# A fused attention, routing and expert kernel: the end of the attention phase in another order

## The chip, the cores and the metric

One core of a Trainium2 chip runs the whole program. The metric is the device time of an execution in microseconds. Five engines work in it, each through its own instructions in order: TensorE (PE; PEld is its weight load), VectorE (DVE), ScalarE (ACT), GpSimd (POOL) and SyncE (SP), which here issues most DMA transfers. They wait for each other through semaphores.

## The reference, cut

Three stages, each with the output of the one before as its input. First a gated linear attention over 4 batches, 8 heads, 768 positions, 40 values a head:

```python
m_new = np.maximum(f_gate[:, :, t] + m, i_gate[:, :, t])
C = f_stab * C + i_stab * np.einsum('bhd,bhe->bhde', vt, kt)
n = f_stab * n + i_stab * kt
h_tilde = np.einsum('bhde,bhe->bhd', C, qt)
denom = np.maximum(np.abs(nq), 1.0)
y[:, :, t] = sigmoid(o_gate) * h_tilde / denom
```

Then a mixture of 8 experts on the 3072 tokens of 320 values, where each token goes to one expert, and a gated layer with 1536 hidden values:

```python
e_idx = np.argmax(x @ w_gate, axis=1)
out[mask] = gate_w * eom * (np.maximum(x[mask] @ w1[e], 0.0) @ w2[e])
return (sigmoid(x @ w_gate) * (x @ w_val)) @ w_out
```

## The kernel before, in words

The tokens are cut into 24 chunks of 128 (six chunks a batch). The attention runs as a pipeline of steps: `step(n)` goes through the names in the table `ORDER` (lines 40 to 43), each with a lag, and calls the part of that name for chunk n minus lag. All five engines run in the order in which the code issues (a manual schedule). For a chunk the parts are, in the order in which its data needs them: `dec`, `exp`, `sc`, `pf` (the products of queries and keys with their decay), `kw`, `inter`, `state`, `C`, `Cm`, `cb` (the running state), `gs` and `out` (the chunk's result in PSUM), `abs` and `den` (the denominator and its reciprocal), `th` (ScalarE, tanh of the output gate), `th1` (adds one to it, line 743, 128x320 in float32), `sod` (GpSimd: gate times reciprocal), `x` (VectorE), `xh`, `xla`, `xl` (the row as a high and a low half: ScalarE, GpSimd, VectorE), `tr` and `ev` (five transposes and their copy out of PSUM), `log` and `lg` (the logits).

When the logits of a group of chunks are there (groups of 6, 6, 4, 5 and 3 chunks), `route` (line 783) computes for its tokens the expert, the row within the expert's list and the gate, as a generator of small pieces, most of them VectorE ops, which `r` entries of `ORDER` pull one by one; a piece that yields `True` ends the entry, since the next one waits for another engine. Its one-hot table (L802) goes to TensorE (L806, L808), whose counts the later pieces read. Behind it the chunk's rows are `pending`, and `scatter` (line 848) writes the rows of one chunk into the experts' lists in DRAM by an indirect DMA that GpSimd issues (L850), one a step at `scat`, and more through `out_of` in later steps.

The first 16 chunks choose the first expert (the one with most tokens), and its first 256 rows are handled by a job of its own, `Head`: its rows are loaded by a transposing DMA (L337, with the small L338 behind it) once the scatters of the first 16 chunks have landed, `sums` (L879 on VectorE, L880 on ScalarE) adds their halves, `up` (L888) makes 24 float32 matmuls, three for each of eight blocks of hidden values, with a relu on ScalarE behind each block (L890), and `down` (L894) makes 16. `load_weights` loads that expert's weights through SP in six blocks, at the steps that `LOADS` names, and `convert` splits them into halves for the expert's remaining rows (L111 on ScalarE, L112 on VectorE). SP also writes blank rows behind the expert's list (`blank_rows`, L101).

Before, steps 1 to 25 run; steps 24 and 25 finish the last chunks with what is left of `ORDER`. In step 23 the early rows' load is issued, in step 24 `sums` and the first 12 matmuls of `up`. Then `tail` runs the route of chunks 16 to 20 to its end, the pending scatters, `tr`, `ev`, `log` and `lg` of chunks 21, 22 and 23 one after the other, the last route, `sort_experts`, the last scatters, the conversion and `down`. The remaining rows of the first expert follow as the next job: its matmuls (L125) need the second load of rows, which waits for all scatters and for `sort_experts`. The other experts and the gated layer come behind.

## Time and profile before

| | |
|---|---|
| median of 3 runs | 727.23 us (726.78 to 731.73) |
| the profiled execution: its time, its span | 726.39 us, 724.3 us |
| TensorE busy, matmuls | 698.8 us (96%) |
| VectorE busy | 396.7 us (55%) |
| ScalarE busy | 328.1 us (45%) |
| GpSimd busy | 144.8 us (20%) |
| mean granted TensorE clock | 0.981 |

The span runs from the first to the last instruction; times within it count from its start. "Busy" is the time in which an engine worked on an instruction; TensorE's matmuls are pipelined and their ends are modelled, so that a busy TensorE need not be at its peak. The granted clock is TensorE's, 1.00 being 2.4 GHz. A wait is named by the instruction that ended it.

### The profile page before, as it was taken

The page shows a single profiled execution, that of the slowest core. Times are in us where ns is not written, and L with a number is a line of the kernel's source. Part 1 is how long each engine was busy: PE and PEld are TensorE (multiplying, and loading weights), DVE is VectorE, ACT ScalarE, POOL GpSimd, SP SyncE. Part 2 cuts the span into 40 slices and gives each one's busy share as a digit, 9 for nine tenths or more (in the row PEclk, how much of TensorE's full clock was granted, in tenths as well). Part 3 has the DMA queues.
Part 4 walks back from the last instruction along what each step waited for, and adds up shares of the span by engine and source line. Part 5 has one row for each costly group of instructions (what it writes and reads, how often), then busy time and mean ns, then how long its engine had stood idle before and what let it go on. Part 6 is the DMA issues. An engine that isn't in the chain of part 4 may idle for free. (4 is left out here: it accounts for less than half of the span.)

```text
span 724.3 us, 15451 instructions
## 1 busy us (share of the span) xinstructions
PE 698.8 (96%) x6048; PEld 495.2 (68%) x6048; DVE 396.7 (55%) x912; ACT 328.1 (45%) x782; POOL 144.8 (20%) x172
## 2 busy tenths in 40 slices
PE   8899999869999999999989999999999999999998
PEld 5799998857666775667656676666666666666665
DVE  6767678627788879898877810322403223032230
ACT  5477787625575666654545511322313223132231
POOL 5456788842211121221100000000000000000000
PEclk8799999988999999999999999999999999999999
DMA  6466667543999998873525013001020020000000
GB/s 192 130 183 178 199 185 215 174 143 87 273 297 292 266 274 234 253 232 108 139 59 138 21 35 76 0 19 37 1 55 1 10 47 1 28 1 10 19 0 28
DMA packets 67131, 84.02 MB, mean 116 GB/s; under 512 B 41401, under 2 KB 48970, under 8 KB 67058
## 3 DMA queue, kind: packets, MB, share of 16 engines
q1 hardware_dynamic: 63824, 73.35, 36.1%
q0 software_dynamic: 2640, 9.33, 3.6%
q8 instruction: 48, 0.79, 0.5%
q10 hardware_dynamic: 594, 0.35, 0.2%
q14 instruction: 25, 0.20, 0.1%
HBM read 57.53 MB, written 17.16 MB: 103 GB/s over the span
## 5 line engine op out<-in xcount | busy, mean ns | idle before, releaser
L125 PE MATMUL pa<-xT,wgv 128*128 128x384 f16 x1536 | 250.9, 326 | 2.8 <-DVE hh L1166 2.1
L125 PEld LDWEIGHTS <-wgv 128*128 128x128 f16 x1536 | 150.2, 98 | 102.2 <-issue 3.4
L1161 DVE SCALAR_TENSOR_TENSOR gt<-pa,sg 128x384 f32<-128x384 f32 x96 | 53.5, 557 | 224.2 <-PE pa L125 193.3
L1179 PE MATMUL pb<-wo,hh 128*128 128x320 f16 x864 | 118.5, 299 | 0.0
L1160 ACT ACTIVATE sg<-pa 128x384 f32<-128x384 f32 x96 | 47.0, 490 | 143.7 <-PE pa L125 143.7
L1179 PEld LDWEIGHTS <-hh 128*128 128x128 f16 x864 | 84.5, 98 | 33.2
L358 PE MATMUL pb<-w,hh 128*128 128x320 f16 (+4 forms) x624 | 86.6, 299 | 0.0
L125 PE MATMUL pa<-xT,w 128*128 128x384 f16 (+5 forms) x576 | 80.9, 301 | 1.6 <-DVE hh L348 1.6
L358 PEld LDWEIGHTS <-hh 128*128 128x128 f16 (+4 forms) x624 | 62.8, 101 | 22.3 <-DVE hh L348 0.5
L125 PEld LDWEIGHTS <-w 128*128 128x128 f16 x640 | 55.7, 98 | 32.6 <-issue 2.6
L112 DVE SCALAR_TENSOR_TENSOR w<-ws,w 128x512 f16<-128x512 f32 (+1 forms) x92 | 56.1, 642 | 4.7 <-ACT w L111 3.9
L111 ACT ACTIVATE w<-ws 128x512 f16<-128x512 f32 (+1 forms) x92 | 50.3, 592 | 13.1 <-DMA ws<-in_w 11.7
L1181 ACT ACTIVATE ob<-pb 128x320 f32<-128x320 f32 x24 | 10.5, 437 | 100.5 <-PE pb L1179 100.5
L660 PE MATMUL ps<-qk 128*128 128x128 f32 x384 | 53.9, 287 | 0.0
L1166 DVE TENSOR_TENSOR hh<-gt,hh 128x384 f16<-128x384 f32 x96 | 52.7, 549 | 0.7
L369 POOL DMA_INDIRECT y_d<-yr,own x24 | 28.0, 1167 | 125.0 <-ACT w L111 19.5
L1165 ACT ACTIVATE hh<-gt 128x384 f16<-128x384 f32 x96 | 49.4, 515 | 5.9 <-DVE gt L1161 5.9
L660 PEld LDWEIGHTS ps<-qk 128*128 128x128 f32 x384 | 49.9, 203 | 1.0 <-issue 0.2
L665 DVE TENSOR_TENSOR pf<-ps,w 128x512 f32<-128x512 f32 x48 | 33.0, 686 | 21.7 <-ACT w L655 11.4
L347 ACT ACTIVATE hh<-pa 128x384 f16<-128x384 f32 (+6 forms) x80 | 33.4, 431 | 13.8 <-PE pa L125 13.1
L348 DVE SCALAR_TENSOR_TENSOR hh<-pa,hh 128x384 f16<-128x384 f32 (+6 forms) x80 | 36.3, 480 | 3.9 <-ACT hh L347 3.6
L655 ACT ACTIVATE w<-pw 128x512 f32<-128x512 f32 x48 | 28.3, 592 | 1.4 <-PE pw L651 0.5
(185 smaller groups left out, 716.5 us busy)
## 6 DMA issues: line engine op xcount, KB each, us to landing
ws<-in_w SPq DMA_DIRECT2D x24, 512.0 KB
vk<-in_vk SPq DMA_DIRECT2D x24, 324.0 KB
qk<-in_qk SPq DMA_DIRECT2D x48, 160.0 KB
ws<-in_w SPq DMA_DIRECT2D x15, 480.0 KB
ws<-in_wg SPq DMA_DIRECT2D x9, 512.0 KB
ws<-in_wv SPq DMA_DIRECT2D x9, 512.0 KB
ws<-in_wo SPq DMA_DIRECT2D x8, 480.0 KB
out<-ob SPq DMA_DIRECT2D x24, 160.0 KB
```

Source lines behind the costliest of these rows:

```text
L111: A.activation(hi, src, AF.Copy, scale=scale)
L112: low = lambda: V.scalar_tensor_tensor(lo, src, scale, hi, ALU.mult, ALU.subtract)
L125: PE.matmul(ps, r if swap else l, l if swap else r, start=n == 0, stop=n == len(steps) - 1)
L347: A.activation(self.hh[:, 0, f], ph, AF.Relu)
L348: V.scalar_tensor_tensor(self.hh[:, 1, f], ph, 0.0, self.hh[:, 0, f], ALU.max, ALU.subtract)
L358: PE.matmul(py, self.hh[:, x, k, sl], w2[:, y, k, :], start=k == 0 and x + y == 0, stop=k == K1 - 1 and x == 1)
L660: PE.matmul(m.ps[g][:, p, :], m.k2[:, g, p], m.q2[:, p], start=True, stop=True)
L1160: A.activation(sg, pgv[0], AF.Sigmoid, scale=1.0 / (SY * SWG))
L1161: V.scalar_tensor_tensor(gt, pgv[1], SGT / (SY * SWV), sg, ALU.mult, ALU.mult)
L1165: A.activation(self.gh[:, 0, f, :], box[0], AF.Copy)
L1166: V.tensor_sub(self.gh[:, 1, f, :], box[0], self.gh[:, 0, f, :])
L1179: PE.matmul(po, self.gh[:, x, k, sl], wo[:, y, k * DM:(k + 1) * DM], start=k == 0 and x + y == 0, stop=k == K2 - 1 and x == 1)
```

## The change

- `th1` (line 743) runs on VectorE instead of GpSimd, for all 24 chunks.
- From step 17 on a second scatter a step is issued behind `xla`; the extra ones behind `kw` and `sod` of the last steps are gone, and `r` and `scat` are no longer left out in step 23.
- The early rows' load is issued in step 22, behind `xl`'s place, and with it the blank rows' write, which before came in step 24. `LOADS` puts the third, fourth and fifth block of weights in step 23 (before 23, 24, 24), the sixth in `tail` (before step 25). `sums` runs at the end of step 23.
- Steps 24 and 25 are gone. `tail` is written out: what is left of the chunks 21 to 23 (`c`, `d`, `e`), pieces of the route of chunks 16 to 20 and single matmuls of `ups` in turn. `up(n)` issues n matmuls, `r(n)` n pieces of a route, `posts()` the relus due.

```diff
         def th1(m):
-            G.tensor_scalar_add(gate(m.t)[:, 0], gate(m.t)[:, 0], 1.0)
+            V.tensor_scalar_add(gate(m.t)[:, 0], gate(m.t)[:, 0], 1.0)
...
-            def up(self, f):
...
-                return lambda: A.activation(self.hh[:, f], ph, AF.Relu, scale=SW1 * SW2)
+            def ups(self):
+
+                for f in range(K1):
...
+                    for k in range(3):
+                        PE.matmul(ph, step.ws[k][:, 128 * f:128 * (f + 1)], self.x32[:, k], start=k == 0 and f % 2 == 0, stop=k == 2,
+                                  skip_group_check=True)
+                        if k == 2:
+                            step.posts.append(lambda f=f, ph=ph: A.activation(self.hh[:, f], ph, AF.Relu, scale=SW1 * SW2))
+                        yield
...
-                    if n == NTILE - 1 and name == "xl":
-
+                    if n == NTILE - 2 and name == "xl":
+
+                        assert not pending
                         mem = Within(hids[0], psS, psC, ("pw", "c"))
                         step.job = Head(mem, step.row, HEAD, lambda ins: tc.add_to_no_dep_group("first rows", ins.ins))
+
+                        blank_rows(first_end(), SLOTS[0] - HEAD)
                     parts[name](chunks[n - lag])
...
-                    if n >= (NTILE - 1 if name != "sod" else 20) and name in ("kw", "sod", "xla"):
+                    if n >= 17 and name == "xla":
                         out_of(1)
...
+            if n == NTILE - 1:
+                step.job.sums()
...
+            c, d, e = chunks[-3:]
...
+            load_weights(5)
+            th(e)
+            gs(e)
+            sod(d)
+            tr(c)
+            ev(c)
+            th1(e)
+            r(2)
+            for g in range(2):
+                out_(e, g)
+            log(c)
+            lg_(c)
+            x(d)
+            abs_(e)
+            den(e)
+            xh(d)
+            up(2)
+            r(3)
+            sod(e)
+            xla(d)
+            xl(d)
+            r(3)
+            up(3)
+            x(e)
+            xh(e)
+            r(4)
+            xla(e)
+            xl(e)
+            tr(d)
+            ev(d)
+            up(2)
+            tr(e)
+            log(d)
+            lg_(d)
+            for _ in step.route:
+                pass
+            ev(e)
             out_of(len(pending))
...
+            up(2)
+            log(e)
+            lg_(e)
+            r(5)
+            up(3)
+            posts()
+            r(3)
+            up(3 * K1)
+            for _ in step.route:
                 pass
             sort_experts()
             out_of(len(pending), True)
+            posts()
             convert(len(step.pieces))
...
-        LOADS = {21: [0], 22: [1], 23: [2], 24: [3, 4], 25: [5]}
+        LOADS = {21: [0], 22: [1], 23: [2, 3, 4]}
...
-            for n in range(1, NTILE + 2):
+            for n in range(1, NTILE):
                 step(n)
             tail()
```

What stands on the engines now, at three places. First GpSimd's own order in steps 21 and 22. L850 is a scatter, L673 `kw`, L758 `xla`, L743 `th1`, L737 `sod`. Before, from `kw` of step 21 on:

```order
L673 TENSOR_TENSOR kw_113<-vk,tm 128x8x40
L850 DMA xs_d<-xsb,dest 29824x322
L758 TENSOR_TENSOR xsb<-x,xsb 128x256
L743 TENSOR_SCALAR hh<-hh 128x320
L737 TENSOR_TENSOR sod<-hh,den 128x320
L850 DMA xs_d<-xsb,dest 29824x322
L673 TENSOR_TENSOR kw_112<-vk,tm 128x8x40
L850 DMA xs_d<-xsb,dest 29824x322
```

And in the change:

```order
L673 TENSOR_TENSOR kw_113<-vk,tm 128x8x40
L850 DMA xs_d<-xsb,dest 29824x322
L758 TENSOR_TENSOR xsb<-x,xsb 128x256
L850 DMA xs_d<-xsb,dest 29824x322
L737 TENSOR_TENSOR sod<-hh,den 128x320
L673 TENSOR_TENSOR kw_112<-vk,tm 128x8x40
L850 DMA xs_d<-xsb,dest 29824x322
```

`th1` is gone from this engine, and a scatter stands in its place behind `xla`; the one behind `sod` is gone.

Then SP's queue in steps 22 and 23: L432 loads a chunk's values, L910 (L913 in the change) a block of the first expert's w1, L337 and L338 the early rows, L917 (L920) a block of its w2, L101 writes the blank rows. Before:

```order
L432 DMA vk<-in_vk 128x648
L910 ISA
L910 DMA ws<-in_w 128x1024
L910 ISA
L910 DMA ws<-in_w 128x1024
L337 ISA
L337 DMA_TRANSPOSE hh<-xs_d 128x5x256
L338 ISA
L338 DMA hh<-xs_d 128x2x2
L917 ISA
L917 DMA ws<-in_w 128x960
```

And in the change:

```order
L913 DMA ws<-in_w 128x1024
L337 ISA
L337 DMA_TRANSPOSE hh<-xs_d 128x5x256
L338 ISA
L338 DMA hh<-xs_d 128x2x2
L250 TENSOR_LOAD first_i
L250 ISA x2
L101 ISA
L101 DMA xs_d<-fill 128x2x322
L913 ISA
L913 DMA ws<-in_w 128x1024
L920 ISA
```

The early rows' load has moved ahead of the third block of w1, and the blank rows' write stands between the two.

Last, TensorE around the last route: L888 (L889 in the change) are matmuls of the hidden layer of the first 256 rows, L806 and L808 the counts of the last route, L894 (L897) the output matmuls of those rows. Before:

```order
L888 MATMUL pa<-hh,ws 128x256 x3
L806 LDWEIGHTS c_74
L806 MATMUL pr<-oh,c_74 128x24
L808 LDWEIGHTS c_74
L808 MATMUL pr<-oh,c_74 128x24
L808 LDWEIGHTS c_74
L808 MATMUL pr<-oh,c_74 128x16
L808 LDWEIGHTS c_74
L808 MATMUL pr<-oh,c_74 128x8
L888 MATMUL pa<-hh,ws 128x256 x3
L894 MATMUL pb<-ws,hh 128x320 x3
```

And in the change:

```order
L889 MATMUL pa<-hh,ws 128x256 x3
L806 LDWEIGHTS c_74
L806 MATMUL pr<-oh,c_74 128x24
L808 LDWEIGHTS c_74
L808 MATMUL pr<-oh,c_74 128x24
L808 LDWEIGHTS c_74
L808 MATMUL pr<-oh,c_74 128x16
L808 LDWEIGHTS c_74
L808 MATMUL pr<-oh,c_74 128x8
L889 MATMUL pa<-hh,ws 128x256 x12
L897 MATMUL pb<-ws,hh 128x320 x3
```

Twelve of the 24 hidden-layer matmuls stand behind the last route now, where three did.

## Rows read from the trace of the kernel before

**Rows 1.** Busy time by stretch: us, then the engines, TensorE's granted clock, DMA.

```profile
142.40:147.80 5.40, 1.14 (x34) 1.03 (x33) 1.75 (x4) 0.84 (x5) 1.73 (x2) 0.96 0.74 115
147.80:151.00 3.20, 3.18 (x8) 2.63 (x9) 1.84 (x7) 0.49 (x3) 2.41 (x3) 0.54 0.56 226
...
161.00:164.00 3.00, 0.08 (x2) 0.00 (x0) 0.00 (x0) 0.89 (x2) 1.17 (x4) 0.50 0.30 110
164.00:167.50 3.50, 3.46 (x19) 2.74 (x20) 1.48 (x9) 1.07 (x5) 0.00 (x0) 0.50 0.02 5
...
177.50:724.30 546.80, 539.06 (x3665) 353.21 (x3664) 277.13 (x567) 213.92 (x460) 35.09 (x28) 1.00 0.35 99
```

**Rows 2.** Order of time, step 23 on: start us, us, engine, line [idle before <-releaser].

```profile
142.46 0.51 DVE L698 TENSOR_TENSOR po<-po,tm 128x328 f32<-128x328 f32 x1
...
142.71 1.49 SPq L337 DMA_TRANSPOSE hh<-xs_d  x1
...
143.02 1.13 PE L683 MATMUL po<-vk,pf 128*64 128x41 f32 x32 [0.61 <-DVE po L698]
...
147.02 0.69 DVE L879 TENSOR_TENSOR hh<-hh 128x512 f32<-128x512 f16 x1 [2.14 <-DMA hh<-xs_d]
...
148.89 0.15 DVE L732 TENSOR_SCALAR den<-den 128x8 f32<-128x8 f32 x1
...
151.47 0.71 POOL L758 TENSOR_TENSOR xsb<-x,xsb 128x256 f16<-128x256 f32 x1 [1.10 <-ACT xsb L755]
...
154.67 2.84 PE L888 MATMUL pa<-hh,ws 128*128 128x256 f32 x12
...
157.34 0.44 PE L767 MATMUL pt<-c,xsb 128*128 128x128 f16 x5
...
158.98 0.18 ACT L778 ACTIVATE lg<-pl 128x16 f32<-128x16 f32 x1 [0.45 <-PE pl L125]
...
163.28 0.70 ACT L771 ACTIVATE xTu<-pt 128x640 f16<-128x640 f16 x1 [2.04 <-remote]
...
164.68 0.18 DVE L792 TENSOR_REDUCE m<-lg 128x3 f32<-128x24 f32 x1 [8.74 <-ACT lg L778]
...
165.54 0.18 DVE L802 TENSOR_TENSOR oh<-rk,m 128x24 f16<-128x24 f32 x1
...
167.13 1.87 PE L888 MATMUL pa<-hh,ws 128*128 128x256 f32 x6
...
168.84 1.78 PE L894 MATMUL pb<-ws,hh 128*128 128x320 f32 x6
...
177.54 7.15 PE L125 MATMUL pa<-hh,w 128*128 128x256 f16 x64
```

**Rows 3.** GpSimd's groups from 120 to 138 us: busy us, mean ns | idle.

```profile
L743 POOL TENSOR_SCALAR hh<-hh 128x320 f32<-128x320 f32 x4 | 4.1, 1014 | 0.1
L758 POOL TENSOR_TENSOR xsb<-x,xsb 128x256 f16<-128x256 f32 x4 | 2.7, 687 | 1.1 <-ACT lg L778 0.7 <-ACT m L817 0.3
...
L737 POOL TENSOR_TENSOR sod<-hh,den 128x320 f32<-128x320 f32 x3 | 2.2, 722 | 0.2
```

**Rows 4.** Order of time in steps 22 and 23, columns as in rows 2.

```profile
136.26 1.03 POOL L850 DMA_INDIRECT xs_d<-xsb,dest  x1 [0.17 <-issue]
...
136.64 0.68 DVE L732 TENSOR_SCALAR den<-den 128x8 f32<-128x8 f32 x1
...
138.05 0.28 PE L767 MATMUL pt<-c,xsb 128*128 128x128 f16 x2 [0.59 <-POOL xsb L758]
...
139.94 1.05 POOL L850 DMA_INDIRECT xs_d<-xsb,dest  x1 [0.16 <-issue]
```

**Rows 5.** Two lines by themselves: ns min/median/max, first and last start, forms.

```profile
L732 DVE TENSOR_SCALAR den<-den x24: 149/392/677, 28.6 to 148.9; 128x8 f32<-128x8 f32 x24
L1097 DVE TENSOR_SCALAR u<-ws x26: 403/419/591, 227.3 to 414.9; 128x512 uint32<-128x512 uint32 x18, 128x480 uint32<-128x480 uint32 x8
```

**Rows 6.** VectorE's group of `pf` from 40 to 138 us: busy, mean ns | idle.

```profile
L665 DVE TENSOR_TENSOR pf<-ps,w 128x512 f32<-128x512 f32 x39 | 26.8, 686 | 14.7 <-ACT w L655 10.2 <-PE pw L651 3.8 <-issue 0.3
```

More of the change, by code (lines that the diff above doesn't have):

```diff
@@ L859, in routing @@
             for _ in range(k):
-                if next(step.route, None) and not step.drain:
+                if next(step.route, None):
                     break
@@ L880, in sums @@
                 A.activation(self.x32[:, 2], self.xT[:, 2], AF.Copy)
-            def up(self, f):
-                if f % 2 == 0:
-                    self.both = psS.tile([128, NP * T], F32, name="pa", tag=("pw", "ps")[f // 2 % 2]).rearrange("p (f n) -> p f n", f=2)
-                ph = self.both[:, f % 2]
-                for k in range(3):
-                    PE.matmul(ph, step.ws[k][:, 128 * f:128 * (f + 1)], self.x32[:, k], start=k == 0 and f % 2 == 0, stop=k == 2,
-                              skip_group_check=True)
-                return lambda: A.activation(self.hh[:, f], ph, AF.Relu, scale=SW1 * SW2)
+            def ups(self):
+                for f in range(K1):
+                    if f % 2 == 0:
+                        both = psS.tile([128, NP * T], F32, name="pa", tag=("pw", "ps")[f // 2 % 2]).rearrange("p (f n) -> p f n", f=2)
+                    ph = both[:, f % 2]
+                    for k in range(3):
[4 more added lines that the diff above has]
+                        yield
             def products(self, w2, i, py):
@@ L927, in step @@
         def step(n):
-            step.drain = n >= NTILE
             if n == 3:
@@ L958, in step @@
                         to_end(1)
-                    if n >= (NTILE - 1 if name != "sod" else 20) and name in ("kw", "sod", "xla"):
+                    if n >= 17 and name == "xla":
                         out_of(1)
-                    if n == NTILE and name == "x":
-                        step.job.sums()
-                    if n == NTILE and name == "out1":
-                        step.posts, step.done = [step.job.up(f) for f in range(4)], 0
+            if n == NTILE - 1:
+                step.job.sums()
@@ L966, in tail, with up @@
         def tail():
-            def ups(n):
+            step.posts = []
+            ups = step.job.ups()
+            c, d, e = chunks[-3:]
+            def up(n):
                 for _ in range(n):
-                    step.posts.append(step.job.up(len(step.posts)))
-            def posts(n):
-                for p in step.posts[step.done:n]:
-                    p()
-                step.done = n
-            stops = 0
-            for stop in step.route:
-                if stop:
-                    stops += 1
-                    if stops == 2:
-                        ups(UPS - len(step.posts))
-                        posts(2)
@@ L984, in tail, with posts @@
-            out_of(len(pending))
-            for t in (NTILE - 3, NTILE - 2, NTILE - 1):
-                tr(chunks[t])
-                ev(chunks[t])
-                log(chunks[t])
-                if t == NTILE - 2:
-                    posts(UPS - 2)
-                lg_(chunks[t])
-            ups(1)
-            posts(UPS)
-            for stop in step.route:
-                pass
-            ups(1)
-            posts(K1)
+                    next(ups, None)
+            def posts():
+                while step.posts:
+                    step.posts.pop(0)()
@@ new lines, in r @@
+            def r(n):
+                for _ in range(n):
+                    next(step.route, None)
+            load_weights(5)
[17 more added lines that the diff above has]
+            sod(e)
```

15 lines of the change are left out of this document (5 added, 10 removed).

## The prediction, before the run

> **What bounds the kernel now.** I read the table of stretches first. From 177.5 us to the end TensorE is busy 539.06 of 546.80 us at a granted clock of 1.00; ahead of that it has holes, with 1.14 us of work in the 5.40 from 142.4 on and 0.08 in the 3.00 from 161 on [rows 1]. So what follows the attention runs at TensorE's pace, and the change can only move the moment at which that long stretch begins: the first matmul of the first expert's remaining rows (L125), at 177.54 [rows 2]. The profiled execution took 726.39 us, which is 177.54, plus 546.8 behind it, plus some 2.1 outside the span.
>
> Then I read the order of time from step 23 to 177.54 [rows 2], as one chain. Chunk 23's `gs` (L698) starts at 142.46 and its `out` matmuls (L683) end at 144.15. Then VectorE sits 2.14 us in front of `sums` (L879, 147.02), because the first expert's rows, asked for at 142.71, have not landed; behind `sums` in VectorE's queue stand `xl` of chunk 22 and `den` and `x` of chunk 23. Twelve of TensorE's 24 hidden-layer matmuls (L888; in float32, each leaves two records) and the route of chunks 16 to 20 follow, and only then, at 157.34, the transposes of chunk 21, with 22 and 23 behind them one at a time. ScalarE then loses 2.04 us to a release that the profile calls remote (163.28). The last one-hot (L802) ends at 165.72, the last three hidden-layer matmuls (six records) start at 167.13, the 16 output matmuls (L894) at 168.84, and L125 at 177.54. TensorE's granted clock is 0.54 from 147.8 to 151 and 0.50 from 161 to 167.5 [rows 1], each time after it had little to do; 0.50 is the level of 1.2 GHz.
>
> **The sum, in the same chain.** Everything is counted to the start of L125.
>
> *Steps 1 to 22.* `th1` goes from GpSimd (1.01 us each, L743 [rows 3]) to VectorE. No row has it there. The nearest is a one-input op on 128x512 at 403 ns, and a 128x8 op of the same kind takes 149 ns alone [rows 5]; a line between them gives 0.31 us for 320 columns, an estimate. In a plain step its cover is VectorE's own wait for ScalarE's `w`, 14.7 us over 39 `pf` ops, about 0.75 us a step (two `pf` ops of 0.38 each) [rows 6]; it stands right behind `den`, ahead of `gs`, `C` and `pf0`. Where that cover is gone (the steps in which a route runs, and the first two) it costs its whole 0.31. I count eight such steps up to 20, but the pieces of a route partly fall in other gaps, and I take 0.8 us (bounds 0 and 2.5).
>
> In the late steps GpSimd has two scatters (1.03 [rows 4]), `th1` 1.01, `sod` 0.72, `kw` (of `sod`'s shape, taken alike) and `xla` 0.69 [rows 3]: 5.2 us of work, and TensorE's transposes wait on `xla`, 0.59 us in step 23 [rows 4]. Without `th1` it is 4.2 us. So the two scatters a step from the 17th fit, and this wait goes (bounds of the gain 0 and 1.4, twice such a wait and some): I take 0.6. Net of both: 0.2 us later at step 23.
>
> *The first expert's rows.* The last of the 16 early scatters stands at 139.94, in step 23 [rows 4]. With two a step it moves into step 22, some 5 us earlier, and their load (142.71, 2.77 us behind that scatter's start) to about 138. They landed 4.31 us after their issue (147.02 minus 142.71) [rows 2], so at about 142.3. `sums` now stands ahead of `gs` of chunk 23 on VectorE, as does `th1` of chunk 22. `gs` moves from 142.46 to 142.46 + 0.31 + 0.69 + 0.2 = 143.7, and the rows are there by then: the 2.14 us wait goes, and nothing takes its place.
>
> *From `gs` of chunk 23 to the last one-hot.* The bare chain from before's rows [rows 2]: `gs` to the end of `out`, 142.46 to 144.15, 1.7; `abs` 0.3 (an estimate from `den`'s 0.15 and a handover); `den` to the end of `xla`, 148.89 to 152.18, 3.3, less 0.3 for a `th1` that `sod` waited for there; transposes to logits, 157.34 to 159.16, 1.8; five route pieces, 164.68 to 165.72, 1.05. Together 7.9. On the same engines chunk 22's `x`, `ev`, `log`, `lg` and the pieces of the first of the two routes go ahead: I add 2.0 (bounds 0, if all of it falls in the waits, and 4, which also covers a stall like the remote one's 2.04). The hidden-layer matmuls that are put between cost TensorE 0.41 each (six of them, 12 records, from 154.67 to some 0.2 before the next op's start at 157.34), at most three in a row, and stand where it would wait. So the last one-hot ends at 143.7 + 9.9 = 153.6, instead of 165.72.
>
> *From there to L125.* 0.5 for the route's matmuls. Then 12 hidden-layer matmuls stand behind the last route, where before it were 3: 12 x 0.41 = 4.9. Then the output matmuls, 168.84 to 177.54, 8.7, unchanged. One weight block now is loaded behind the early rows and the blank rows on SP's queue, and its third matmul may stand for it: 0.3 (bounds 0 and 2). L125 starts at 153.6 + 0.5 + 4.9 + 8.7 + 0.3 = 168.0. The other inputs of L125 (scatters of the last three chunks, the plan, the second load of rows, the weights' conversion) took at most 177.54 - 165.72 = 11.8 us from the last one-hot; here there are 14.4, so they stay hidden with some 2 us to spare.
>
> So 177.54 - 168.0 = 9.5 us less: 716.9 for an execution like the profiled one. The median of before, 727.23, is 0.84 above that execution, so I give **717.7 us**.
>
> **A rule against it.** `den` (128x8 on VectorE) takes 149 ns at best, 392 in the median and 677 at most [rows 5]. In step 22 it starts at 136.64 inside a scatter that runs from 136.26 to 137.29, and it ends at 137.32, right behind it [rows 4]. The Trainium skill, *SBUF — State Buffer*, "Who interferes with whom", says why: a one-input VectorE op in its two-port mode and GpSimd exclude each other for a whole instruction, and the one that issues second waits. By that rule `th1` on VectorE can stand for the second scatter, which now follows `xla` directly. The trace agrees for that `den`; for an op of `th1`'s size no run here shows it yet. By the rows alone the price is bounded by `den`'s excess, 677 - 149 = 0.53 us a step. The sum above leaves it out: in the changed order that scatter starts behind `xla`, when `den` is already under way, and the bulk of its wait is paid in before's steps as well. If each `th1` met the scatter, the sum would be the first rival's.
>
> **Rivals.**
>
> 1. *VectorE pays for `th1` in the late steps.* `th1` waits out the scatter in the five steps 17 to 21, in which one follows `xla`, at 0.31 + 0.53 each: 717.7 + 4.2 = 721.9. For: `den`'s long cases [rows 5]. Against: VectorE's 0.75 us of waiting a step [rows 6].
> 2. *The clock.* TensorE has many short jobs in the tail, and before it fell to 0.50 twice there [rows 1]. If it is at the lower level when the 12 matmuls behind the last route run, they take 0.82 each: 4.9 more, 722.6. Against: in the chain above TensorE works some 75% of the time from 144 on, and its longest pause is about 2 us, where before it had 1.14 us of work in 5.4.
> 3. *The rows do not come sooner.* If the last early scatter or its load stays near 142.7 (SP's or GpSimd's queue holds it), `sums` stays at 147.0, and as it now stands ahead of `gs`, the chain starts at 147.7 instead of 143.7: 717.7 + 4.0 = 721.7.
> 4. *Slower.* `th1` lies on the step's loop (`den`, `th1`, `gs`, `C`, `Cb`, `inter`) in all 23 steps. At 0.31 alone that is 7 us and only eats the gain; with `den`'s excess, 0.84 a step, it is 19 us: 727.2 - 9.5 + 19.3 = 737. It decides from 9.5/23 = 0.41 us a step on, and gives a clear loss from 0.73. Against: before's VectorE waits 0.75 us for `w` in each step [rows 6] and TensorE had no wait there that VectorE could lengthen, except in steps with a route.
>
> **How the numbers follow.** The forecast gets 0.66, rival 1 0.13, rival 2 0.09, rival 3 0.06, rival 4 0.06. The forecast's own range: 713.8 with its additions at their good ends (2.0 of queueing, 0.8 of `th1`, 0.8 more relief, 0.3 of the weight block), 721.4 with the queueing at 4 and the weight block at 2. The range 713.5 to 722.5 takes in rivals 1 and 3 and, as its size is rough, half of rival 2. One per cent, about what a measurement of this kernel can tell from no change, is 7.3 us: below 719.96 lies nine tenths of the forecast and a little of the rivals, 0.62. Slower by over 1%: 0.06. The rest, 0.32, is within.
>
> **What would show it.** In the profile after: the early rows' load (L337) issued near 138 and `sums` with no or little wait; `th1` on VectorE at about 0.31 us, and late steps no longer than before's; no wait of the transposes for `xla` in steps 22 and 23; the last one-hot near 153.6; 12 matmuls at 0.41 behind it at full clock; L125 near 168. If `th1` takes 0.8 in the late steps, rival 1 is right; a granted clock of 0.5 behind the last route shows rival 2; a wait ahead of `sums` rival 3; a wider distance of the steps all along rival 4. If the last one-hot lies near 153.6 and L125 later than 169.5, the spare time of the scatters or of the conversion was mis-sized.

## The result and the profile after

The changed kernel takes **718.11 us** in the median of four runs (716.55 to 719.8), beside 727.0 us (725.06 to 731.73) for the kernel before on the same chip: a ratio of 0.9886, with a 95% interval of 0.9852 to 0.9921. A second set of six runs, on another chip, gave 716.53 us against 723.6, a ratio of 0.9887 (0.9849 to 0.9925). So the change takes 1.1% off, some 8 us.

| | before | after |
|---|---|---|
| the profiled execution: its time, its span | 726.39 us, 724.3 us | 718.95 us, 717.2 us |
| TensorE busy, matmuls | 698.8 us | 694.8 us |
| VectorE busy | 396.7 us | 403.7 us |
| GpSimd busy | 144.8 us | 116.3 us |
| mean granted TensorE clock | 0.981 | 0.990 |

VectorE has 7.0 us more, which are 24 `th1` of 0.29, and GpSimd 28.5 us less, of which 24 of 1.01 make the most. The rows that answer to [rows 2], after's order of time from step 22 on (start, duration, engine, line, operation, and in brackets the idle time before it and what ended it):

```profile
137.65 1.39 SPq L337 DMA_TRANSPOSE hh<-xs_d  x1
...
141.37 0.69 DVE L879 TENSOR_TENSOR hh<-hh 128x512 f32<-128x512 f16 x1 [1.34 <-DMA hh<-xs_d]
141.97 0.50 DVE L698 TENSOR_TENSOR po<-po,tm 128x328 f32<-128x328 f32 x1
...
142.53 1.59 PE L683 MATMUL po<-vk,pf 128*64 128x41 f32 x32 [2.53 <-DVE po L698]
...
143.50 0.36 SPq L913 DMA_DIRECT2D ws<-in_w  x1
...
148.32 1.56 PE L889 MATMUL pa<-hh,ws 128*128 128x256 f32 x6 [1.83 <-DMA ws<-in_w]
149.72 0.44 PE L767 MATMUL pt<-c,xsb 128*128 128x128 f16 x5
...
152.76 0.36 PE L125 MATMUL pl<-wgl,xTu 128*128 128x16 f16 x8 [0.25 <-ACT xTu L771]
152.98 1.54 PE L889 MATMUL pa<-hh,ws 128*128 128x256 f32 x6
...
154.79 0.18 ACT L778 ACTIVATE lg<-pl 128x16 f32<-128x16 f32 x1 [2.08 <-PE pa L889]
155.86 0.18 DVE L802 TENSOR_TENSOR oh<-rk,m 128x24 f16<-128x24 f32 x1
156.22 5.43 PE L889 MATMUL pa<-hh,ws 128*128 128x256 f32 x24
161.48 1.78 PE L897 MATMUL pb<-ws,hh 128*128 128x320 f32 x6
...
170.09 1.15 PE L125 MATMUL pa<-hh,w 128*128 128x256 f16 x9
```

What to see: the early rows (L337) are asked for at 137.65, where it was 142.71, and `sums` (L879) comes ahead of `gs` (L698). The transposes of chunk 21 are done before 142 (they stood at 157.34), those of 22 start at 149.72, and the last one-hot ends at 156.04 instead of 165.72. But three waits are left that the forecast had at nothing or, for the block, at 0.3: 1.34 us for the rows, 1.83 for the third block of hidden-layer weights (L913, asked for at 143.50 behind the rows and the blank rows), and 2.08 ahead of the last logits' eviction (L778). The block is asked for late because SP, which issues in order, stands in front of the blank rows' write (L101, at 142.86) until the early rows' second load (L338) has landed, 2.1 us in after and 0.8 in a2, the second execution of the changed kernel (after's waits of SP: us in total, times, longest):

```profile
SPq L101 <- DMA hh<-xs_d: 2.1, 1, 2.1
```

The rows that answer to [rows 1], after's table of stretches (us, then busy time of the engines, the clock, DMA):

```profile
142.50:148.30 5.80, 3.96 (x50) 3.25 (x50) 4.28 (x20) 1.75 (x7) 1.73 (x3) 0.71 0.75 204
148.30:156.00 7.70, 5.95 (x46) 4.55 (x46) 1.49 (x9) 2.23 (x7) 5.72 (x11) 1.00 0.57 223
156.00:170.10 14.10, 14.00 (x61) 10.76 (x62) 12.66 (x48) 8.47 (x21) 3.12 (x5) 1.00 0.33 96
170.10:717.20 547.10, 540.35 (x3665) 353.99 (x3663) 275.17 (x557) 214.47 (x460) 31.56 (x28) 1.00 0.34 98
```

From L125 on these two traces hardly differ: 547.10 us with 540.35 of TensorE's work, before 546.80 with 539.06. So between them the whole gain lies ahead of L125. That does not hold for every pair of runs, as e2 below shows.

**Not all of the two traces' difference is the change.** The first half of the attention runs the same instructions but for `th1`, yet the transposes of chunk 2 start at 46.60 us before and at 44.08 after. From the start on, the clock granted to TensorE differs from execution to execution; these are the rows from 10 to 20 us of before, of after, of the run e1 and of e9:

```profile
10.00:20.00 10.00, 9.24 (x80) 7.55 (x80) 6.72 (x12) 2.62 (x6) 3.97 (x4) 0.66 0.69 188
10.00:20.00 10.00, 9.29 (x109) 7.18 (x109) 7.41 (x14) 2.62 (x6) 3.92 (x4) 0.83 0.67 192
10.00:20.00 10.00, 7.84 (x109) 6.19 (x109) 8.47 (x17) 2.62 (x6) 4.52 (x5) 1.00 0.63 189
10.00:20.00 10.00, 9.21 (x70) 7.61 (x70) 6.72 (x13) 2.62 (x6) 4.00 (x4) 0.59 0.68 188
```

Over fourteen profiled executions the start of chunk 2's transposes lies between 44.0 and 47.4. To keep this out, traces are compared below by distances from that start (46.60 before, 44.08 after): to `gs` of chunk 23, to the end of the last one-hot, to the start of L125; each is the difference of two starts in the order of time. "Behind" is the span from L125 on, and the sum of the last two is what the times should follow.

| kernel | `gs` (23) | last one-hot | L125 | behind | sum |
|---|---|---|---|---|---|
| before | 95.9 | 119.1 | 130.9 | 546.8 | 677.7 |
| after | 97.9 | 112.0 | 126.0 | 547.1 | 673.1 |
| after, second execution (a2) | 96.4 | 109.2 | 123.3 | 546.7 | 670.0 |
| e1, `th1` back on GpSimd | 95.9 | 108.7 | 122.8 | 544.6 | 667.4 |
| e2, `th1` alone | 94.7 | 114.3 | 126.1 | 551.0 | 677.1 |
| e3, `th1` and rows | 94.9 | 117.1 | 127.6 | 546.7 | 674.3 |
| e4, `th1` and tail | 94.7 | 108.7 | 122.7 | 549.4 | 672.1 |
| e6, third block first | 98.3 | 109.8 | 123.8 | 545.9 | 669.7 |
| e7, `sums` behind `gs` | 94.9 | 110.2 | 124.3 | 546.2 | 670.5 |
| e8, eight behind the route | 96.7 | 107.3 | 121.8 | 550.7 | 672.5 |
| e9, e6, e7 and e8 in one | 95.7 | 105.1 | 120.1 | 547.4 | 667.5 |
| e10, `th1` twice | 98.7 | 110.2 | 124.3 | 548.1 | 672.4 |
| e11, e6 and e7 in one | 95.7 | 105.2 | 121.1 | 546.2 | 667.3 |
| e12, e11 and six evictions more | 95.1 | 104.4 | 118.9 | 550.5 | 669.4 |

One execution's distance has incidents of a microsecond or two in it, so a verdict needs the medians beside it, and these resolve some 0.35% (2.5 us).

### The profile page after: what moved, and what is told of

Read it like the earlier page. It is cut to its first block, busy times and chain, and to the rows that moved or that the text cites. A ratio compares the mean times of both kernels' runs of the same rounds, so it can differ in the third digit from the quotient of the medians.

```text
span 717.2 us, 15449 instructions
## 1 busy us (share of the span) xinstructions
PE 694.8 (97%) x6048; PEld 490.4 (68%) x6048; DVE 403.7 (56%) x936; ACT 328.1 (46%) x782; POOL 116.3 (16%) x148
## 5 line engine op out<-in xcount | busy, mean ns | idle before, releaser
L125 PE MATMUL pa<-xT,wgv 128*128 128x384 f16 x1536 | 252.6, 327 | 2.8 <-DVE hh L1198 2.1
L125 PEld LDWEIGHTS <-wgv 128*128 128x128 f16 x1536 | 150.8, 98 | 103.2 <-issue 5.0
L125 PE MATMUL pa<-xT,w 128*128 128x384 f16 (+5 forms) x576 | 80.7, 301 | 0.7 <-DVE hh L348 0.7
L125 PEld LDWEIGHTS <-w 128*128 128x128 f16 x640 | 55.7, 98 | 31.4 <-issue 1.2
L660 PE MATMUL ps<-qk 128*128 128x128 f32 x384 | 51.5, 278 | 0.9 <-DMA qk<-in_qk 0.9
L660 PEld LDWEIGHTS ps<-qk 128*128 128x128 f32 x384 | 47.2, 194 | 2.3 <-issue 1.6
L348 DVE SCALAR_TENSOR_TENSOR hh<-pa,hh 128x384 f16<-128x384 f32 (+6 forms) x80 | 36.3, 479 | 5.2 <-ACT hh L347 5.0
L683 PE MATMUL po<-vk,pf 128*64 128x41 f32 x768 | 27.8, 234 | 2.5 <-DVE po L698 2.5
```

Source lines behind the costliest of these rows:

```text
L125: PE.matmul(ps, r if swap else l, l if swap else r, start=n == 0, stop=n == len(steps) - 1)
L348: V.scalar_tensor_tensor(self.hh[:, 1, f], ph, 0.0, self.hh[:, 0, f], ALU.max, ALU.subtract)
L660: PE.matmul(m.ps[g][:, p, :], m.k2[:, g, p], m.q2[:, p], start=True, stop=True)
```

## The experiments

**e1, e2: `th1` by itself.** e1 gives it back to GpSimd in the changed kernel; e2 moves it in the kernel before.

```diff
-            V.tensor_scalar_add(gate(m.t)[:, 0], gate(m.t)[:, 0], 1.0)
+            G.tensor_scalar_add(gate(m.t)[:, 0], gate(m.t)[:, 0], 1.0)
```

> The changed kernel with th1 given back to GpSimd, nothing else. Its own median is 718.1 us. Theory (th1 on VectorE costs the plain steps nothing and only takes load off GpSimd where there are two scatters a step): GpSimd has some 5.2 us of work in a step of 4.9 us from the 17th on, so the late steps grow by some 0.3 us each and the transposes wait for xla again: 719.5, between 718.5 and 721. Rival (th1 on VectorE lies on the loop of every step, 0.3 us in 23 steps, and the rest of the change is worth that much more): 711 to 713. Rival (GpSimd holds the late steps fully, each scatter and th1 in line, and the rows come later too): 723 to 726.

> The kernel before (727.0 us) with th1 on VectorE, nothing else. Theory (hidden in VectorE's waits, a little relief in the late steps): 726.5, between 725.5 and 727.5, steps as far apart as before. Rival (th1 waits for GpSimd's port or lies on the loop of the steps): 730 to 737. Rival (th1 alone brings a good part of the gain): 724 or less.

Measured: e1 719.05 us, 0.9917 of before (0.9884 to 0.995); e2 723.22, 1.0005 (0.9978 to 1.0033), beside 724.16 for before on the same chip. So `th1` alone changes nothing that can be measured, as its theory said. e1 lies where its theory put it, 0.3% above the changed kernel's 0.9886, but within the intervals, and its trace shows its theory in part: the transposes wait for `xla` again, three times and 1.3 us in all (never in after), and the two steps ahead of chunk 21's transposes are 5.6 and 5.1 us long, a2's 4.9 and 4.5. But the step from chunk 17's transposes to chunk 18's is 0.8 us shorter than a2's, and its `gs` is no later than after's.

e2's L125 stands 4.8 us nearer than before's (126.1 to 130.9). Of this, 2.0 are a stall of ScalarE in before's execution (163.28 [rows 2]), and 4.2 of the 4.8 are given back behind L125. 24 us on, TensorE waits 2.05 us there for VectorE's L348, which stands behind the conversion of the next expert's weights (before waits 0.94), and its clock over the 5 us behind this wait is 0.65:

```profile
194.08 4.44 PE L125 MATMUL pa<-xT,w 128*128 128x384 f16 x16 [2.05 <-DVE hh L348]
```

The instruction itself, in after on VectorE and in e1 on GpSimd, and `den` in after (ns, shortest, median, longest):

```profile
L743 DVE TENSOR_SCALAR hh<-hh x24: 274/289/329, 27.0 to 142.4; 128x320 f32<-128x320 f32 x24
...
L743 POOL TENSOR_SCALAR hh<-hh x24: 1004/1012/1548, 26.8 to 141.6; 128x320 f32<-128x320 f32 x24
...
L732 DVE TENSOR_SCALAR den<-den x24: 157/339/892, 26.1 to 144.8; 128x8 f32<-128x8 f32 x24
```

No `th1` on VectorE took over 0.33 us, though with two scatters a step it starts inside one. After's order of time, `th1` beside a scatter, and `den` beside `xla` (L758):

```profile
125.07 1.01 POOL L850 DMA_INDIRECT xs_d<-xsb,dest  x1 [0.15 <-DVE den L732]
125.23 0.28 DVE L743 TENSOR_SCALAR hh<-hh 128x320 f32<-128x320 f32 x1
...
102.77 0.70 POOL L758 TENSOR_TENSOR xsb<-x,xsb 128x256 f16<-128x256 f32 x1 [1.75 <-ACT lg L778]
102.86 0.64 DVE L732 TENSOR_SCALAR den<-den 128x8 f32<-128x8 f32 x1
```

`th1` runs inside the scatter as if it were alone; `den` ends with `xla`, which started just ahead of it.

**e3, e4: rows and tail apart.** e3 is the kernel before with `th1` on VectorE, the scatters of the changed kernel, and the first expert's and the blank rows asked for in step 22; e4 is the changed kernel with the rows, the blank rows, the scatters and the last three weight blocks where they stood before, and `sums` behind `x(d)` in the tail.

The first piece is e3's, in `step(n)` of the kernel before, the second e4's, in `tail()` of the changed one.

```diff
-                    if n == NTILE - 1 and name == "xl":
+                    if n == NTILE - 2 and name == "xl":
...
+                        blank_rows(first_end(), SLOTS[0] - HEAD)
...
-                    if n >= (NTILE - 1 if name != "sod" else 20) and name in ("kw", "sod", "xla"):
+                    if n >= 17 and name == "xla" or n >= NTILE and name in ("kw", "sod"):
```

```diff
             x(d)
+            step.job.sums()
             abs_(e)
```

> The kernel before with th1 on VectorE, two scatters a step from the 17th, and the first expert's rows and the blank rows asked for a step sooner; the order of the tail as before, with sums behind x of chunk 22. Theory (the rows' wait of 2.14 us goes, the rest of the gain is the tail's order): the early rows' load near 138 us, no wait ahead of sums, 724.5, between 723.5 and 726. Rival (the rows carry the change, since all that waits on them moves with them): 720 or less. Rival (the wait only passes to the third weight block, now behind the rows on SP's queue): 726 to 727.5.

> The changed kernel with the first expert's rows, the blank rows and the late scatters where they stood before (rows asked for in step 23, sums behind x of chunk 22 in the tail, one scatter a step), so th1 and the tail's order alone. Theory (the order carries most; sums at about 147 holds den, xl and x of chunk 23 behind it on VectorE, so some 3 us of it are lost): 721.5, between 720 and 723. Rival (the order is worth nothing without the rows, since everything in it queues behind sums): 725 to 727. Rival (the rows are of no use, their wait is taken elsewhere): 717.5 to 719.

Measured: e3 722.74 us, 0.9979 (0.9956 to 1.0002); e4 720.03, 0.9918 (0.9885 to 0.995). The tail's order carries the gain; the sooner rows alone bring at most 0.4%. In e3 the rows came without a wait, but TensorE then stood for the third weight block, whose request had moved behind them (e3's TensorE):

```profile
147.20 7.00 PE L888 MATMUL pa<-hh,ws 128*128 128x256 f32 x20 [3.35 <-DMA ws<-in_w]
```

This is the rival that e3's expectation names, that the wait passes to the block (the time lies between the theory's and its own); the ten matmuls behind it (20 records) took 7.00 us where ten take 4.1 at 0.41. In e4 `sums` waits for the rows until 145.0, and TensorE 2.68 us for `sums`, but its third block is there: it reaches L125 as soon as the second execution of the changed kernel (122.7 and 123.3 us).

**a2: the changed kernel once more.**

> The changed kernel itself once more, so that the next three can be read beside it. Two things are looked for. Where the executions differ: theory, the clock granted to TensorE in the first 40 us (0.66 to 1.00 between 10 and 20 us in the executions seen so far) moves the whole program by up to some 3 us, so the distance from the third set of transposes to the start of the first expert's remaining rows is the same within 1 us from execution to execution, and the median is 718 with a ratio of 0.987 to 0.992. And ScalarE's stall of 2.08 us ahead of the last logits' eviction: theory, it is an incident of that one execution, as the four experiments before it have none at that place, and this distance is then near 124 and not 126.0. Rival: it belongs to this order, the eviction waits for the three matmuls behind the logits, and 2 us stand there again.

Measured: 716.53 us, 0.9887. Its tail has no stall ahead of the last logits' eviction (ScalarE, then TensorE):

```profile
152.48 0.18 ACT L778 ACTIVATE lg<-pl 128x16 f32<-128x16 f32 x1 [0.45 <-PE pl L125]
...
141.43 1.13 PE L683 MATMUL po<-vk,pf 128*64 128x41 f32 x32 [1.91 <-DVE po L698]
...
146.15 2.93 PE L889 MATMUL pa<-hh,ws 128*128 128x256 f32 x6 [1.61 <-DMA ws<-in_w]
148.88 0.74 PE L767 MATMUL pt<-c,xsb 128*128 128x128 f16 x5
...
152.30 1.54 PE L889 MATMUL pa<-hh,ws 128*128 128x256 f32 x6
153.80 0.19 PE L806 MATMUL pr<-oh,c 128*128 128x24 f16 x1
```

The three matmuls at 152.30 run until 153.8, and the eviction starts at 152.48: it does not wait for them. So the 2.08 us of the first execution are an incident, as are the 2.04 of before [rows 2]: e2 and e3, with the same tail, have none there. The wait for the third block is there again, 1.61 us, and now the three matmuls behind it take 2.93 us instead of 1.54: the clock granted from 146 to 149 is 0.50, the lower level. It had fallen ahead of that wait (0.50 from 143.2 to 146 too), behind the 1.91 us in which TensorE waited for `gs`. In after it is the same wait, 2.53 us long, that the lower clock follows (0.50 from 143.0 to 146.4); at the block it is back at 1.00. Without the incident the two executions of this kernel (126.0 and 123.3) agree within the 1 us expected; with it they do not.

**e6, e7: the block, and `sums`, one at a time.**

The first piece is e6's, the second e7's.

```diff
-        LOADS = {21: [0], 22: [1], 23: [2, 3, 4]}
+        LOADS = {21: [0], 22: [1, 2], 23: [3, 4]}
```

```diff
-            if n == NTILE - 1:
-                step.job.sums()
...
             th1(e)
+            step.job.sums()
             r(2)
```

> The changed kernel with the third block of the first expert's hidden-layer weights asked for ahead of the early rows and the blank rows on SP's queue, not behind them. Theory (TensorE's 1.83 us of waiting for that block at 148.3 holds the transposes of chunk 22 and all behind them): 1.7 us less than the changed kernel beside it, about 716.4 where that one is 718.1. Rival (the rows come 0.6 to 1.2 us later for it, gs of chunk 23 stands behind sums and moves with them, and takes it back): within 0.5 us of the changed kernel.

> The changed kernel with sums behind gs and th1 of chunk 23 on VectorE, not ahead of them. Theory (the rows' wait of 1.34 us and the 0.69 of sums no longer hold gs, but the third weight block, asked for behind the blank rows, still holds TensorE until 148.3): gs of chunk 23 some 2 us sooner, the last one-hot and the end within 0.5 us of the changed kernel. Rival (the chain from gs on sets the tail, the weight block follows): 1.5 to 2 us less, about 716.4 where the changed kernel is 718.1.

Measured: e6 717.99 us, 0.9921 (0.9889 to 0.9953); e7 716.48, 0.9892 (0.9859 to 0.9924); the changed kernel beside them 716.53. Neither is faster. In e6 (VectorE, then TensorE) the block's wait is gone, but the rows, asked for at 136.62, landed only at 141.64, 5.0 us later, and `gs` and `out` stood behind them:

```profile
141.64 0.69 DVE L879 TENSOR_TENSOR hh<-hh 128x512 f32<-128x512 f16 x1 [2.69 <-DMA hh<-xs_d]
...
142.81 1.94 PE L683 MATMUL po<-vk,pf 128*64 128x41 f32 x32 [3.88 <-DVE po L698]
```

The outcome is the rival's, its reason hardly: the block had been asked for at 126.71, 10 us ahead of the rows, and in e12, with the same order on SP's queue, the rows were there 3.6 us after they were asked for. Other executions of these kernels in which they were waited for had them in 3.5 to 4.4 us. Why they took 5.0 here stays open. Behind the wait of 3.88 us the clock is 0.50 until 149, so that `out` took 1.94 us where a2's took 1.13. In e7 `gs` is 1.5 us sooner, and TensorE gives it all to the block:

```profile
148.64 2.90 PE L889 MATMUL pa<-hh,ws 128*128 128x256 f32 x6 [3.86 <-DMA ws<-in_w]
```

The time is what its theory said. The last one-hot is not within its 0.5 us but 1.0 later than a2's: from that wait until 152.7 the clock is 0.50.

**e8: eight matmuls behind the last route, not twelve.**

```diff
             up(2)
+            posts()
             tr(e)
...
-            r(5)
             up(3)
             posts()
-            r(3)
+            up(4)
+            r(8)
```

> The changed kernel with seven hidden-layer matmuls between the last logits and the last route's matmuls, not three, so that eight stand behind the route, not twelve; for that the first two relus go a few instructions sooner on ScalarE. Theory (these four lie in TensorE's wait of 1.58 us for the route and come off the end at 0.41 us each): 1.6 us less than the changed kernel, about 716.5 where that one is 718.1. Rival (ScalarE's relus ahead of the last transposes' eviction hold the chain by their 0.66, or the rest of the work before the first expert's rows becomes the bound): within 0.7 us of the changed kernel.

Measured: 719.54 us, 0.9926 (0.9895 to 0.9956): not faster but 3.0 us above a2, more than the rival's 0.7, though the intervals overlap. Yet its L125 stands 1.5 us nearer (121.8 to a2's 123.3); what follows it is 4.0 us longer (550.7 to 546.7). TensorE's order shows why:

```profile
151.03 3.27 PE L889 MATMUL pa<-hh,ws 128*128 128x256 f32 x14
154.14 0.18 PE L806 MATMUL pr<-oh,c 128*128 128x24 f16 x1
...
166.99 7.15 PE L125 MATMUL pa<-hh,w 128*128 128x256 f16 x64 [0.43 <-DMA hh<-xs_d]
191.10 4.44 PE L125 MATMUL pa<-xT,w 128*128 128x384 f16 x16 [2.64 <-DVE hh L348]
```

The last one-hot is there at 152.47, but the route's own matmuls (L806) start at 154.14, behind the seven. So the last scatters do not come sooner, and the first expert's remaining rows and the next expert's weights, which are asked for behind them, do not either: L125 waits 0.43 us for the rows, and 24 us on TensorE stands 2.64 us. The scatters, and what is asked for behind them, have become the bound, which is the second of the rival's two reasons.

**e11, e9: both waits at once.** e11 is e6 and e7 in one, e9 adds e8.

> Two edits in one on the changed kernel: the third hidden-layer weight block ahead of the early rows on SP's queue, and sums behind gs and th1 of chunk 23 on VectorE. Theory (the two waits cover for each other: with the block early gs stands for the rows, with gs early the matmuls stand for the block; with both gone the last route and the last scatters come some 3 to 4 us sooner, so nothing behind is late): distance from the third set of transposes to the first expert's remaining rows 119.5 to 120.5 in place of 123.3, the time 713 where the changed kernel is 716.5. Rival (the first expert's rows land when they land, and the hidden layer behind them sets the tail): distance 122.5 or more, 715.5 to 717.

> Three edits in one on the changed kernel: the third hidden-layer weight block ahead of the early rows, sums behind gs and th1 of chunk 23, and seven hidden-layer matmuls ahead of the last route's own matmuls (eight behind). Distances are from the third set of transposes to the start of the first expert's remaining rows; 123.3 us in the second execution of the changed kernel. Theory (the rows and the block each cover for the other, so only both edits free the tail; the seven matmuls hold the last route's matmuls and so the last scatters by some 1.5 us, and the next expert's weights then come late): distance 118 to 120, but about 2 us of it lost behind, 714.5 where the changed kernel is 716.5. Rival (all three add up): 712 or less. Rival (the scatters' chain is the bound, nothing is left to win): 716 to 718.

Measured, on a chip where before took 729.32 us: e11 714.48 us, 0.9796 (0.9755 to 0.9837); e9 715.25, 0.9801 (0.9759 to 0.9843). Their intervals lie below the changed kernel's 0.9852 to 0.9921. So the two waits did cover for each other, and e8's edit adds nothing to them. With both gone TensorE's clock does not fall there either: from 140 to 160 us it is 1.00 in e9, e11 and e12. The last one-hot is 4 us nearer than a2's (105.2 to 109.2), as expected; L125 is only 2.2 us nearer in e11's trace (121.1, where 119.5 to 120.5 was expected), because ScalarE stood still (ScalarE, then TensorE):

```profile
160.75 1.21 ACT L892 ACTIVATE hh<-pa 128x256 f32<-128x256 f32 x4 [7.95 <-PE pb L897]
...
161.19 2.42 PE L897 MATMUL pb<-qk,hh 128*128 128x320 f32 x8 [1.62 <-ACT hh L892]
```

**e12: e11 with six more ScalarE instructions far ahead.**

```diff
-            A.activation(m.xT, m.pt, AF.Copy)
+            for xs in (slice(0, 3), slice(3, XB)) if m.t in range(4, 10) else (slice(0, XB),):
+                A.activation(m.xT[:, xs], m.pt[:, xs], AF.Copy)
```

> The third weight block ahead of the early rows and sums behind gs and th1, as in the version with these two edits, and beside them six more ScalarE instructions far ahead of the tail (the eviction of the transposes of chunks 4 to 9 in two parts each), which have a cover in ScalarE's idle time of those steps. Looked for: ScalarE stood still for 2 us or more in four of the eleven profiled executions, with its inputs long there, and each time at an instruction within some eight places of each other in its program. Theory (it is tied to the place in ScalarE's instruction stream): if it stands still at all, then at an instruction six places earlier, from the exp of the route of chunks 16 to 20 to the last logits' eviction, between 147 and 153 us. Rival (tied to the time and to what the rest does then): at the same relus as in the version without the six instructions, near 155 to 161 us. No stall in this execution would leave it open. The time in either case as without the six: ratio to before 0.978 to 0.983.

Measured: 714.09 us beside 725.43 for before on its chip, 0.9833 (0.9793 to 0.9873), the upper edge of what was expected; no stall on ScalarE, so the question stays open. But this is the tail without incidents (TensorE, then ScalarE):

```profile
145.03 1.54 PE L890 MATMUL pa<-hh,ws 128*128 128x256 f32 x6
146.41 0.44 PE L767 MATMUL pt<-c,xsb 128*128 128x128 f16 x5
...
151.21 5.43 PE L890 MATMUL pa<-hh,ws 128*128 128x256 f32 x24
156.48 1.78 PE L898 MATMUL pb<-ws,hh 128*128 128x320 f32 x6
...
165.52 7.15 PE L125 MATMUL pa<-hh,w 128*128 128x256 f16 x64 [0.26 <-DMA hh<-xs_d]
188.72 2.76 PE L125 MATMUL pa<-xT,w 128*128 128x384 f16 x16 [1.73 <-DVE hh L348]
...
154.09 0.66 ACT L893 ACTIVATE hh<-pa 128x256 f32<-128x256 f32 x2 [2.15 <-PE pa L890]
```

L125 stands at 118.9, 4.4 us nearer than a2's, and its next bounds show: it waits 0.26 us for its rows, and TensorE later 1.73 us for work behind the next expert's weights. In e12 the relus of the third pair start at 154.09, some 3 us behind the route's one-hot; in e11 they started 8.9 us behind it.

**e10: `th1` twice.** Two operations of 128x320 a step, each adding a half.

```diff
-            V.tensor_scalar_add(gate(m.t)[:, 0], gate(m.t)[:, 0], 1.0)
+            V.tensor_scalar_add(gate(m.t)[:, 0], gate(m.t)[:, 0], 0.5)
+            V.tensor_scalar_add(gate(m.t)[:, 0], gate(m.t)[:, 0], 0.5)
```

> The changed kernel with two VectorE operations of th1's size in each step in place of one (each adds a half). Theory (VectorE waits some 0.75 us a step for ScalarE's w, and th1 takes 0.29 of it, so a second one still fits): plain steps as far apart as before (54.4 us from the third set of transposes to the one fourteen on), at most 0.3 us in each of the eight or so steps in which a route runs, so 716.5 to 719 where the changed kernel is 716.5. Rival (VectorE is on the steps' loop once th1 is there, so the second one costs its 0.29 us in each of 23 steps): the 54.4 us become 57 to 58.5, 722 to 723.5.

Measured: 721.11 us on the chip of e11, 0.9893 (0.9845 to 0.994), so no difference to the changed kernel in time. In the steps there is one: from chunk 2's transposes to chunk 13's it is 56.1 us (102.92 minus 46.84) where both kernels had 54.4. Most of it lies in the two steps that a route makes long (6.1 us in after, 6.9 and 6.8 in e10); the plain ones stay as they were. The start of chunk 13's transposes shows the way, in after and in e10:

```profile
98.44 0.45 PE L767 MATMUL pt<-c,xsb 128*128 128x128 f16 x5 [0.45 <-DVE rows_e L821]
...
102.92 0.45 PE L768 MATMUL pt<-c,xsb 128*128 128x128 f16 x5 [0.81 <-DVE rows_e L822]
```

The route's pieces queue on VectorE behind the second operation, and the transposes wait for the route's buffer. So the cover of 0.75 us holds where no route runs and is used up where one does, between the theory and the rival. All but 1.0 us of it is taken up again by L125 (124.3 to a2's 123.3), since `sums` found its rows there.

## Why the prediction was right, point by point

717.7 us was forecast, and 718.11 and 716.53 were measured: right in time, and the mechanism was the named one, the tail's order in front of L125. Three things were off: the net effect of `th1`, the place of the third weight block, and the stretch behind L125, which the sum held fixed.

- **`th1`: size right, net sign off.** 0.31 us was estimated, 0.289 measured. The plain steps cost nothing: 54.4 us from chunk 2's transposes to chunk 13's in both kernels. The transposes no longer wait for `xla`, as predicted. In place of 0.2 us later, `gs` of chunk 23 comes 1.2 us sooner with `th1` alone (94.7 in e2, 95.9 before), inside the bound of 1.4 for the relief; with two scatters a step it is 94.9 (e3). None of this shows in the medians. The first rival did not come true: `th1` never took more than 0.33 us. The scatter does start behind `den`, as I argued, but `th1` then falls inside it (125.07 and 125.23 above). By my argument that meeting should have brought the first rival's price; it cost nothing. The rule of the Trainium skill that I weighed (*SBUF — State Buffer*, "Who interferes with whom": the second of the two stands for the whole instruction) agrees with `den` beside `xla`, 0.64 us, and not with `th1` in a scatter.
- **The rows: sooner, but less than predicted, and the wait not gone.** 137.65 looks like the predicted 138, but after runs 2.5 us ahead of before from chunk 2 on. Counted from there, the load is asked for at 93.6 in after and 92.2 in a2, where 138 is 91.4 (before: 96.1). It then took 3.72 and 3.55 us, where 4.31 was taken. In after the rows came at 97.3 against a forecast of 95.7, with VectorE there for them at 96.0; in a2 they came as forecast, and VectorE was there at 95.0, sooner than I had it. So a wait of 1.34 and 0.70 us stayed; `gs` at 97.9 and 96.4 against the forecast's 97.1 (143.7 minus 46.60).
- **From `gs` to the last one-hot: the step that failed.** 9.9 us forecast, 14.1 and 12.9 measured. 2.1 of the first is the incident on ScalarE. The rest is the third weight block: the sum had it as 0.3 us behind the last one-hot with a bound of 2, while it stood in the chain ahead of chunk 22's transposes, because the order puts three matmuls there and the first of them needs it. It cost its own 1.6 to 1.8 us and, in a2, 1.4 more since the clock was still at 0.50. The sum named the queue, but not that SP itself would stand for the rows' second load (2.1 and 0.8 us) before it asked for the block. That the rest was sized well is seen in e9, e11 and e12, where the block is early, `sums` stands behind `gs` and the clock stays at 1.00: 9.4, 9.4 and 9.3 us. In e6, with the block early and `sums` ahead of `gs`, it is 11.5, at a clock of 0.50 until 149.
- **Behind the last one-hot: right.** To the first output matmul 5.44 us (161.48 minus 156.04) where 0.5 and 4.9 were forecast, the output matmuls 8.61 where it was 8.7. The clock in this stretch is 1.00, so the second rival's half speed did not happen there; it did ahead, behind TensorE's wait for `gs` (0.50 from 143.0 to 146.4 in after, from 143.2 to 149 in a2). The rival was right that the clock can fall in the new tail, and had the wrong place. I had also read before's second fall as behind the 0.08 us of work in 3.00; that stretch lies at the lower clock already, and ahead of it, from 157.4 to 161, TensorE worked 1.61 of 3.60 us.
- **The spare behind: about right.** Some 2 us were forecast for the other inputs of L125. In neither execution of the changed kernel does L125 wait for one; in e8, with L125 1.5 us nearer and the scatters where they were, it waits 0.43.
- **The sum.** By distances L125 should have come at 121.4 (168.0 minus 46.60); it came at 126.0 and 123.3, so 1.9 us late even without the incident. A gain of 9.5 becomes 7.6. The ratio says 8.2 (1.14% of 724), the medians 8.9 on the first chip and 7.1 on the second, the single traces from 4.6 (677.7 less 673.1) to 7.7 (less 670.0).
- **What the sum did not have.** 2.04 us of its 9.5 are before's stall of ScalarE, an incident and nothing that the change takes away. And it held all behind L125 fixed at 546.8, where the runs have 544.6 to 551.0. e2, with before's tail and no stall, has L125 only 2.8 us behind a2's, and 4.3 more behind it (551.0 to 546.7). Part of this is the wait of 2.05 us at 194.08. In the six executions that wait there (0.9 to 2.6 us: before, e2, e3, e8, e10, e12) the next expert's weights (L189), which SP loads behind the last scatters and the first expert's remaining rows, are asked for 0.9 to 1.3 us behind L125. In the eight that do not, they are asked for between 2.3 us ahead of L125 and 0.3 behind it, in after and a2 1.5 and 2.3 ahead. So bringing L125 forward pays only as far as the last scatters come forward with it. How much of the gain lies behind L125 is not shown, as these are single executions. That the time is met within 0.5 us is luck, since these errors and the relief by `th1` have opposite signs; that the tail's order takes about 1% off is not.

The third rival is refuted by L337, which is asked for 2.5 us (after) and 3.9 (a2) sooner than before by distance; the fourth by the plain steps.

Many of these differences are below what the medians tell apart: e1, e4, e6, e7, e8 and e10 all overlap with the changed kernel. Shown by medians are: `th1` alone nothing, the tail's order some 0.9% (e4 against e2), and the block together with `sums` another 0.5 to 0.9% (e12 and e11; e12's interval still overlaps the changed kernel's, e11's does not). Which part of the tail's order carries its share is not shown, as no run takes it apart. That the sooner rows bring little is seen in e3 and in e4's trace; the 0.3% between e4 and the changed kernel lie within the intervals.

## What to carry to other kernels

When work is put into a gap, everything that this work needs moves with it: here three matmuls, moved ahead of the transposes, brought a weight block's landing into the chain, and the block's request stood behind two others on its queue, of which the second waited for the first to land. Two waits that end at nearly the same time hide each other; taking away either alone shows nothing, and only both show what they cost. Before two traces are compared, find a point ahead of the change at which they should agree, and measure from there.

## What the runs showed of the hardware that was not expected

- The clock granted to TensorE in the first 40 us differs between executions of the same instructions, from 0.58 (e12) to 1.00 (e1) between 10 and 20 us. Chunk 2's transposes start at 44.0 to 47.4. The mean clock over the first 44 us is 0.96 in e1 (44.0) and 0.77 in e9 (47.4), but 0.92 in after (44.1) and in e3 (45.7), so the clock alone does not set it.
- ScalarE stood still in four of fourteen profiled executions for 2 to 6 us with its inputs there: 2.04 us before, 2.08 in after, some 6 us in e11, and twice in e9. Each time it was one of a few neighbouring instructions of its program, near the last logits and the relus behind them. The profile of after names another engine's latest event, which the second execution (a2) shows not to be the reason. Late loading of its instructions is not seen: no packet of a queue that loads instructions lies in the stalls of before, after and e11, and one in e9's. What it is stays open: e12, made to tell the place in the program from the time, had no such stall.
- A scatter does not hold VectorE's `th1`: in after it starts inside one five times, 0.03 to 0.36 us behind the scatter's start, and takes 0.27 to 0.33 us. In e10 the second `th1` starts 0.39 to 0.48 us behind it four times and takes 0.33, as elsewhere; once it starts 0.63 behind and takes 0.49. Yet a `den` that started 0.38 us behind one stood to its end [rows 4]. So the place in the scatter alone does not tell which op is held, and what does stays open.
- The same load of the first expert's early rows lands 3.5 to 5.0 us after its issue, in the eight executions in which VectorE waits for it.
